# Linear attention and two expert layers: a hand-written order changed at the turning of the queries and in the first two steps

## The chip, the cores and the metric

The kernel runs on one NeuronCore of a Trainium2 chip. The metric is the device time of one execution in microseconds (us). Five engines have a queue of their own and run it in order: TensorE (PE in the profile; its weight loads are PEld), VectorE (DVE), ScalarE (ACT), GpSimd (POOL) and SyncE (SP), which here only issues DMA transfers.

## What is computed

```python
def _attn_ref(q, k, v, w_phi):            # q, k, v: (4, 8, 576, 64); w_phi: (64, 128)
    def phi(x):
        proj = np.einsum('bhsd,df->bhsf', x, w_phi)
        proj = proj - np.max(np.abs(proj), axis=-1, keepdims=True)
        return np.concatenate([np.exp(proj), np.exp(-proj)], axis=-1)
    q_p, k_p = (phi(q), phi(k))
    kv = np.einsum('bhsf,bhsd->bhfd', k_p, v)
    z = np.sum(k_p, axis=2)
    num = np.einsum('bhsf,bhfd->bhsd', q_p, kv)
    den = np.einsum('bhsf,bhf->bhs', q_p, z)[..., None] + 1e-06
    return num / den
```

Its output, as a matrix of 2304 tokens by 512, goes through a dense layer (the largest of three products with 512 x 768 matrices, then a product with a 768 x 512 matrix) and through a layer of eight experts of which each token uses two. Only the attention's part of the program is changed.

## The kernel before, in words

The attention is done in 16 steps (`NS`), one for two heads of one batch entry; a pair of steps (an even one and the odd one behind it) has the same two heads of two batch entries. Of the 576 positions 512 are a step's own; the 64 that remain (the remainder) of both steps of a pair are put together into one tile of 128 rows, kind "r", and worked on in the even step.

A step does the following. `turn` (L359) transposes the keys, the queries or the remainder on TensorE into a PSUM bank of `bank_t` (two banks), four transpositions (two for the remainder). `raw_in` (L374) copies that on ScalarE. `proj` (L380) multiplies by `w_phi` into two banks of `bank_p`, one for each group g of four tiles. On VectorE `peak` (L395) takes the largest absolute value of each row and `center` (L402) subtracts it; the subtraction also frees the bank. For keys `exp_k` (L415) makes exp(x) and exp(-x) on ScalarE. Queries are turned back once centred, by `turn_q` (L427) on TensorE, again into `bank_t`, one half (g = 0, g = 1) at a time, and `exp_q` (L434) makes the exponentials on ScalarE, which frees that bank. `kv_sum` (L448) multiplies key features by values (four products and a fifth with the remainder's features for each sign), `kv_out` copies the sums, and `numer` (L465) multiplies them by the query features in four pieces (n, h): three in a row, and the last, (1, 1), in the next period. `denom`, `den_turn`, `den_inv`, `den_back` and `divide` make the output.

The order is written by hand. `at(t, f, ...)` puts a call at a nominal time; all calls are sorted by that number, and the sorted list gives the order of each of the queues of TensorE, ScalarE, VectorE and SyncE. The number does not delay anything: what runs when is set by the queues and the semaphores. `period(base, a, b)` (L539) writes the calls for one period of 12.5: the keys and queries of step a beside the sums and numerators of step b = a - 1. `start` (L512) issues the first loads. During the attention SyncE, VectorE, ScalarE and GpSimd also convert the dense layer's weights (`narrow_load`, `narrow_mid`, `narrow_end`, `narrow_out`); GpSimd's order is the scheduler's. The tiles of transposed input (`th`), of centred values (`d`) and of loaded keys and queries have three buffers each.

Of the kernel before, what the change touches and what calls it, by code (L numbers as in the profile page):

```python
# [11 lines left out]
BF16 = mybir.dt.bfloat16  # L12
# [7 lines left out]
P = 128  # L20
# [3 lines left out]
class Plan:  # L24
# [5 lines left out]
    def at(self, t, f, *x):  # L30
        self.ops.append((t, len(self.ops), f, x))
# [7 lines left out]
def tile_linear_attention__then__moe__then__noisy_top2_moe(  # L39
# [20 lines left out]
    nc = tc.nc  # L60
# [3 lines left out]
    E, _, FF2 = e_w1.shape  # L64
# [26 lines left out]
    at = plan.at  # L91
    st, pools = {}, {}
# [197 lines left out]
    ap, ain = pools["attn"], pools["ain"]  # L290
# [17 lines left out]
    vts, rest, tiles = [], {}, {}  # L308
# [5 lines left out]
    def load_rest(bb):  # L314
        ql = ain.tile([P, H, D], F32, name="ql", bufs=1)
        kl = ain.tile([P, H, D], F32, name="kl", bufs=1)
        for t, src in ((kl, k), (ql, q)):
            for i in range(2):
                rows = slice(i * REST, (i + 1) * REST)
                dq.dma_start(t[rows], src[2 * bb + i, :, MAIN:S, :].rearrange("h p d -> p h d"))  # L320
        rest[bb] = ql, kl

    def load_rest_v(bb):
        for i in range(2):
            rows = slice(i * REST, (i + 1) * REST)
            for s in range(2):
                dq.dma_start(vls[i][rows, :, 2 * s, :],
                             v[2 * bb + i, s:H:2, MAIN:S, :].rearrange("h p d -> p h d"))

    def load_main(s):  # L330
        u, i = divmod(s, 2)
        bb, hp = divmod(u, HP)
        b = 2 * bb + i
        res = []
        for nm, src in (("km", k), ("qm", q)):
            t = ain.tile([P, 2, JT, D], F32, name=nm, bufs=3)
            dq.dma_start(t.rearrange("p h j d -> p h (j d)"),
                         src[b, 2 * hp:2 * hp + 2, 0:MAIN, :]
                         .rearrange("h (p j) d -> p h (j d)", j=JT))
            res.append(t)  # L340
        tiles[s] = res + [vts[s % 3]]

    def load_vals(s):
        u, i = divmod(s, 2)
        bb, hp = divmod(u, HP)
        b = 2 * bb + i
        vt = vts[s % 3]
        for h in range(2):
            dq.dma_start(vt[:, :, 2 * h, :],
                         v[b, 2 * hp + h, 0:MAIN, :].rearrange("(p j) d -> p j d", j=JT))  # L350
# [26 lines left out]
        nc.scalar.activation(t[:, :src.shape[1]], src, AF.Copy)  # L377
        st["t", kind] = t

    def proj(s, kind):  # L380


        t = st["t", kind]
        pj = [bank_p().rearrange("p (a f) -> p a f", a=4) for _ in range(2)]
        for jj in range(2 if kind == "r" else 4):
            for g in range(2):
                rows = slice(g * D, (g + 1) * D)
                nc.tensor.matmul(pj[g][:, jj, :], t[rows, jj, :], wphi[rows], start=True, stop=True)  # L388
        for g in range(2):
            st["pj", kind, g] = pj[g]  # L390
# [114 lines left out]
    NS = B * HP  # L505
# [4 lines left out]
            qps[s // 2, n] = ap.tile([P, 2, 2, S], F32, name=f"qp{n}", tag="qp", bufs=3)  # L510

    def start():  # L512
        warm = ap.tile([P, 1], F32, name="warm")
        nc.vector.memset(warm, 0.0)
        nc.scalar.activation(warm, warm, AF.Exp)
        load_main(0)
        for h in range(2):
            dq.dma_start(wphi[h * D:(h + 1) * D], w_phi)
        make_identity(nc, ident)
        for vt in vts:  # L520
            nc.gpsimd.memset(vt[:, :, 1, :], 1.0)
        for i in range(2):
            nc.gpsimd.memset(vls[i][(1 - i) * REST:(2 - i) * REST], 0.0)
            nc.gpsimd.memset(vls[i][i * REST:(i + 1) * REST, :, 1, :], 1.0)
        load_rest(0)
        load_vals(0)
        load_rest_v(0)
        load_main(1)
        load_vals(1)

    def step_halves(a):

        def count(a):
            return min(a, 1) + (a % 2 if a > 1 else 0)

        n = sum(count(i) for i in range(a))
        return range(n, n + count(a) if a < NS else len(halves))

    def period(base, a, b):  # L539

        def at(t, f, *x):
            plan.at(base + t, f, *x)

        if 0 < a < NS:
            at(0.0, fill, a)
            if a == 3:
                at(0.0, routing_loads)
            if a == 2:
                at(2.0, routing_consts)
            if a + 1 < NS:  # L550
                at(0.0, load_main, a + 1)
                at(0.0, load_vals, a + 1)
        if a < NS:
            if a % 2 == 0:
                at(0.0, prepare, a)
            if a + 1 == 2 * HP:
                at(0.0, load_rest, 1)
            at(0.0, turn, a, "k")
            at(0.5, raw_in, a, "k")
            at(2.7, turn, a, "q")  # L560
            at(3.2, raw_in, a, "q")
            at(3.15, proj, a, "k")
            at(4.0, peak, a, "k", 0)
            at(4.7, center, a, "k", 0)
            at(5.4, peak, a, "k", 1)
            at(6.1, center, a, "k", 1)
            for g in range(2):
                for sg in range(2):
                    at(5.3 + 1.5 * g + 0.6 * sg, exp_k, a, "k", g, sg)
            at(7.25, proj, a, "q")  # L570
            at(8.1, peak, a, "q", 0)
            at(8.8, center, a, "q", 0)
            at(9.5, peak, a, "q", 1)
            at(10.2, center, a, "q", 1)
            at(11.5, turn_q, a, "q", 0)
            at(11.95, turn_q, a, "q", 1)
            at(11.9, exp_q, a, "q", 0)
            at(12.4, exp_q, a, "q", 1)
            if a % 2 == 0:
                late = 0.0 if a else 2.1  # L580
                at(2.8 + late, turn, a, "r")
                at(3.4 + late, raw_in, a, "r")
                at(11.05, proj, a, "r")
                for g in range(2):
                    at(11.5 + 0.01 * g, peak, a, "r", g)
                    at(11.52 + 0.01 * g, center, a, "r", g)
                at(STEP + 3.0, turn_q, a, "r", 0)
                at(STEP + 3.1, exp_q, a, "r", 0)
                at(12.39, exp_k, a, "r", 0, 0)
                at(12.39, exp_k, a, "r", 0, 1)  # L590
            for n in step_halves(a):
                at(1.8 if a > 1 else 11.0, narrow_mid, n)
                at(2.8 if a > 1 else 11.5, narrow_end, n)
                at(STEP + (1.6 if a > 1 else 9.0), narrow_out, n)
            for n in step_halves(a + 1):
                at(8.0, narrow_load, n)
        if 0 < b:
            at(4.05, numer, b - 1, 1, 1)
            at(5.0, denom, b - 1, 1, 1)
            at(5.05, den_turn, b - 1, 1)  # L600
            at(6.05, den_inv, b - 1, 1)
            at(6.8, den_back, b - 1, 1)
            at(7.2, divide, b - 1, 1, 0)
            at(7.6, divide, b - 1, 1, 1)
        if 0 <= b:
# [4 lines left out]
            at(7.3, kv_out, b)  # L610
            at(8.15, numer, b, 0, 0)
# [9 lines left out]
            at(12.1, denom, b, 1, 0)  # L621

    at(0.0, start)
    for s in range(NS):
        period(s * STEP, s, s - 1)
    T = NS * STEP
# [366 lines left out]
    def overflow_table():  # L993
# [16 lines left out]
        for r in range(NREG):  # L1010
# [112 lines left out]
    for i in range(2 * 4):  # L1123
        g, j = 1 + i // 4, i % 4
        t = END + 0.1 + i * 3.2
# [207 lines left out]
```

## Time and profile before

| | |
|---|---|
| median of 3 runs | 1048.41 us (1047.31 to 1049.32) |
| the profiled execution | 1048.3 us |
| its span, first to last instruction | 1046.6 us |
| TensorE busy | 1011.4 us, 97% of the span |
| VectorE, ScalarE, GpSimd busy | 502.6, 383.7 and 314.0 us |
| TensorE busy in the first of 40 slices of the span | 7 tenths; 9 in nearly all others |
| granted TensorE clock, mean | 0.993 |

The span is what one profiled execution shows; the time of the same execution is 1.7 us longer. Busy time of TensorE counts matrix products and transpositions; idle time of the other engines costs nothing unless TensorE waits for them. A row of the timeline can stand for several instructions of one kind in a row (x4); its duration runs from the start of the first to the end of the last, and the ends of products overlap with the next ones' starts. A float32 transposition or product of 128 columns appears as one pass or two.

### The profile page before, as it was taken

The numbers are of one execution on the slowest core, as the hardware profiler recorded it, in microseconds if no ns is written. First come the engines' busy times: TensorE is split into PE (matmuls) and PEld (weight loads), VectorE is DVE, ScalarE is ACT, GpSimd is POOL, SyncE is SP. The second block draws the span as 40 slices with busy tenths as digits, with TensorE's granted clock in tenths as the row PEclk, the third lists the DMA queues.
The fourth block names the chain that finished last, engine by engine and source line by source line (L and its number), as shares of the span: only waits on it lengthen the run. The fifth ranks groups of instructions, "written<-read, shape, count | busy, mean of one in ns | idle before, by whom it ended". The sixth has DMA issues, their size and how long they took to land. (4 is left out here: it accounts for less than half of the span.)

```text
span 1046.6 us, 15778 instructions
## 1 busy us (share of the span) xinstructions
PE 1011.4 (97%) x6154; PEld 904.5 (86%) x6154; DVE 502.6 (48%) x1064; ACT 383.7 (37%) x717; POOL 314.0 (30%) x345
## 2 busy tenths in 40 slices
PE   7999999999999999999998999999999999999995
PEld 6888888889999999999997788989898979898883
DVE  2877777876524242424264616534354444444220
ACT  3666666664322222222244405323131323233110
POOL 2477654454002020202012464323233233220121
PEclk9999999999999999999999999999999999999998
DMA  6264575423300000000125435635343454542010
GB/s 189 60 192 138 146 217 186 139 86 106 96 31 1 31 2 31 1 31 1 56 96 123 149 95 181 214 104 161 114 143 135 135 167 135 159 129 74 25 64 32
DMA packets 78526, 109.21 MB, mean 104 GB/s; under 512 B 33358, under 2 KB 47822, under 8 KB 78450
## 3 DMA queue, kind: packets, MB, share of 16 engines
q1 hardware_dynamic: 67522, 78.57, 25.0%
q0 software_dynamic: 10928, 29.62, 9.1%
q8 instruction: 49, 0.80, 0.3%
q14 instruction: 27, 0.22, 0.1%
HBM read 84.77 MB, written 23.98 MB: 104 GB/s over the span
## 5 line engine op out<-in xcount | busy, mean ns | idle before, releaser
L891 PE MATMUL s<-gx,wh 128*128 128x304 f32 (+1 forms) x960 | 209.1, 309 | 0.6 <-DVE hl L902 0.6
L891 PEld LDWEIGHTS s<-gx,wh 128*128 128x128 f32 x960 | 159.0, 188 | 4.1 <-DVE hl L902 0.9
L891 PE MATMUL s<-gx,wl 128*128 128x304 f32 (+1 forms) x480 | 148.3, 309 | 0.0
L659 PE MATMUL s<-xh,wh 128*128 128x384 f32 x432 | 147.7, 342 | 0.2 <-DVE xT L502 0.2
L659 PE MATMUL s<-xh,wl 128*128 128x384 f32 x432 | 145.4, 337 | 0.0
L659 PE MATMUL s<-xl,wh 128*128 128x384 f32 x432 | 145.2, 336 | 0.0
L822 POOL DMA_INDIRECT meta<-mt,si x36 | 36.5, 1013 | 266.6 <-DVE si L818 257.5
L901 ACT ACTIVATE hh<-s 128x304 fp32r<-128x304 f32 (+1 forms) x120 | 52.1, 434 | 154.2 <-PE s L891 150.7
L122 DVE TENSOR_TENSOR wl<-raw,wh 128x1024 fp32r<-128x1024 f32 x72 | 88.0, 1223 | 40.4 <-ACT wh L121 40.3
L902 DVE SCALAR_TENSOR_TENSOR hl<-s,hh 128x304 fp32r<-128x304 f32 (+1 forms) x120 | 58.1, 488 | 96.0 <-ACT hh L901 95.9
L121 ACT ACTIVATE wh<-raw 128x1024 fp32r<-128x1024 f32 x72 | 76.0, 1056 | 58.7 <-PE p L960 19.6
L669 DVE TENSOR_TENSOR a<-s,a 128x384 f32<-128x384 f32 x72 | 40.1, 557 | 118.9 <-PE s L659 109.6
L891 PEld LDWEIGHTS s<-gx,wl 128*128 128x128 f32 x480 | 90.7, 189 | 1.4
L960 PE MATMUL p<-wh,hh 128*128 128x512 f32 (+1 forms) x216 | 87.0, 403 | 0.0
L960 PE MATMUL p<-wl,hh 128*128 128x512 f32 (+1 forms) x216 | 85.1, 394 | 0.0
L960 PE MATMUL p<-wh,hl 128*128 128x512 f32 (+1 forms) x216 | 84.9, 393 | 0.0
L659 PEld LDWEIGHTS s<-xh,wh 128*128 128x128 f32 x432 | 81.2, 188 | 2.2 <-DVE xT L502 0.6
L659 PEld LDWEIGHTS s<-xl,wh 128*128 128x128 f32 x432 | 81.2, 188 | 1.4
L659 PEld LDWEIGHTS s<-xh,wl 128*128 128x128 f32 x432 | 81.1, 188 | 0.0
L972 POOL DMA_INDIRECT out_dram<-o,emeta x40 | 44.5, 1113 | 119.8 <-DVE o L970 105.6
L398 DVE TENSOR_REDUCE m<-p 128x4 f32<-128x512 f32 (+1 forms) x80 | 49.4, 624 | 50.5 <-PE p L388 50.1
L865 POOL DMA_INDIRECT gx<-x2d,emeta x40 | 38.3, 957 | 109.0 <-PE t L876 100.4
(209 smaller groups left out, 1834.3 us busy)
## 6 DMA issues: line engine op xcount, KB each, us to landing
raw<-in_moe_w_dram SPq DMA_DIRECT2D x64, 512.0 KB, 3.8
bits<-in_moe_w_dram SPq DMA_DIRECT2D x18, 512.0 KB, 4.3
out_dram<-zrow SPq DMA_DIRECT2D x9, 512.0 KB, 5.1
x2d<-x SPq DMA_DIRECT2D x18, 256.0 KB, 2.6
km<-in_k_dram SPq DMA_DIRECT2D x16, 256.0 KB, 5.2
qm<-in_q_dram SPq DMA_DIRECT2D x16, 256.0 KB, 5.6
vt<-in_v_dram SPq DMA_DIRECT2D x32, 128.0 KB, 4.6
narrow<-nm SPq DMA_DIRECT2D x16, 256.0 KB, 2.6
```

The costliest lines, as they stand in the source:

```text
L121: nc.scalar.activation(hi, src, AF.Copy)
L122: nc.vector.tensor_tensor(lo, src, hi.bitcast(F32), op=ALU.subtract)
L398: nc.vector.tensor_reduce(m, st["pj", kind, g][:, :n], axis=AX.X, op=ALU.max, apply_absolute_value=True)
L659: nc.tensor.matmul(p_, a[:, d, fs], b_, start=(n == 0), stop=(n == 3 * KD - 1))
L669: nc.vector.tensor_tensor(a, p_, st.pop("a"), op=ALU.max)
L822: ins = nc.gpsimd.indirect_dma_start(out=meta, out_offset=bass.IndirectOffsetOnAxis(ap=si[:, t, kk:kk + 1], axis=0), in_=mt[:, t, kk, :], ...
L865: nc.gpsimd.indirect_dma_start(out=xg[:m], out_offset=None, in_=x2d[0:nrow, :], in_offset=bass.IndirectOffsetOnAxis(ap=st["meta", n][:m, i ...
L891: nc.tensor.matmul(p_, a[:, fs], b_[:, d, cs], start=(i == 0), stop=(i == 3 * KD - 1))
L901: nc.scalar.activation(hh[:, cs], p_, AF.Relu)
L902: nc.vector.scalar_tensor_tensor(hl[:, cs], p_, 0.0, hh[:, cs].bitcast(F32), op0=ALU.max, op1=ALU.subtract)
L960: nc.tensor.matmul(p_, a[:, cs], b_[:, fw], start=(r == 0), stop=(r == 3 * F2 - 1))
L972: ins = nc.gpsimd.indirect_dma_start(out=out, out_offset=bass.IndirectOffsetOnAxis(ap=mt[:m, i, 1:2], axis=0), in_=o[:m], in_offset=None, ...
```

## The change

1. In every step but the first, the first half of the queries is turned back between the second and the third numerator, and the second half behind the third (nominal times 9.95 and 11.05 instead of 11.5 and 11.95). The exponentials follow at 10.5 and 11.5, both ahead of the third numerator's denominator. The remainder's projection moves from 11.05 to 11.4.
2. The calls for step 0 and for the keys and queries of step 1 up to their projections are no longer written by `period` but by a new function `opening`, in another order: the remainder is turned before the first projection, its projection goes to two idle banks of `bank_s`, and the projection of step 0's queries to one bank of each kind; step 1's keys are turned before step 0's sums.
3. `load_main` can load the keys or the queries alone. The queries of step 0 and the keys of step 1 are loaded behind the remainder, the queries of step 1 behind the values.
4. `busy(n)` multiplies a tile of zeros (`idle`, two-byte numbers, 256 columns) by itself n times into the bank of `bank_k`: 12 times at the beginning, 4 times in front of the first `kv_sum`.

```diff
-    def proj(s, kind):
+    def proj(s, kind, banks=(bank_p, bank_p)):
...
-        pj = [bank_p().rearrange("p (a f) -> p a f", a=4) for _ in range(2)]
+        pj = [bank().rearrange("p (a f) -> p a f", a=4) for bank in banks]
...
     def start():
+        st["idle"] = ap.tile([P, 256], BF16, name="idle")
+        nc.vector.memset(st["idle"], 0.0)
...
-        load_main(0)
+        load_main(0, 0)
...
         load_rest(0)
+        load_main(0, 1)
+        load_main(1, 0)
         load_vals(0)
         load_rest_v(0)
-        load_main(1)
+        load_main(1, 1)
         load_vals(1)
+
+    def busy(n):
+
+        t = bank_k()
+        for _ in range(n):
+            nc.tensor.matmul(t[:, :256], st["idle"][:, :P], st["idle"], start=True, stop=True)
...
-            at(11.5, turn_q, a, "q", 0)
-            at(11.95, turn_q, a, "q", 1)
-            at(11.9, exp_q, a, "q", 0)
-            at(12.4, exp_q, a, "q", 1)
+            at(9.95, turn_q, a, "q", 0)
+            at(10.5, exp_q, a, "q", 0)
+            at(11.05, turn_q, a, "q", 1)
+            at(11.5, exp_q, a, "q", 1)
...
-                at(11.05, proj, a, "r")
+                at(11.4, proj, a, "r")
...
+    def opening():
+
+        at(1.2, busy, 12)
+        at(4.0, turn, 0, "k")
...
+        at(11.0, busy, 4)
...
     at(0.0, start)
+    opening()
```

TensorE at the beginning, before (km and qm are a step's keys and queries, kl and ql those of the remainder; t, p, s and k are the kinds of PSUM bank):

```order
L371 MATMUL t<-ident,km 128x128 x4
L371 MATMUL t<-ident,qm 128x128 x4
L388 MATMUL p<-wphi,th 128x128 x8
L371 MATMUL t<-ident,kl 128x128
L371 MATMUL t<-ident,ql 128x128
L388 MATMUL p<-wphi,th 128x128 x12
L431 MATMUL t<-ident,d 128x128 x8
```

And TensorE at the same place in the changed program, where the lines' numbers are one to a few higher:

```order
L540 MATMUL k<-idle 128x256
L372 MATMUL t<-ident,km 128x128 x4
L372 MATMUL t<-ident,kl 128x128
L372 MATMUL t<-ident,ql 128x128
L389 MATMUL p<-wphi,th 128x128 x8
L372 MATMUL t<-ident,qm 128x128 x4
L389 MATMUL s<-wphi,th 128x128 x4
```

The first row is the last of twelve products of zeros; the remainder's two transpositions stand ahead of the first projection, and the remainder's projection (the last row) goes to banks of kind s.

TensorE at the end of a period with an even step a, before (the six rows of L469 are numerators of the step ahead, qp the query features, d centred values, vt and vl values):

```order
L388 MATMUL p<-wphi,th 128x128 x8
L469 MATMUL s<-qp_395,kv 128x288 x6
L388 MATMUL p<-wphi,th 128x128 x4
L431 MATMUL t<-ident,d 128x128 x8
L371 MATMUL t<-ident,km 128x128 x4
L457 MATMUL k<-vt_109,kp_837 128x128 x4
L457 MATMUL k<-vl_111,kp_923 128x128
```

And TensorE there in the changed program:

```order
L389 MATMUL p<-wphi,th 128x128 x8
L470 MATMUL s<-qp_156,kv 128x288 x4
L432 MATMUL t<-ident,d 128x128 x4
L470 MATMUL s<-qp_156,kv 128x288 x2
L432 MATMUL t<-ident,d 128x128 x4
L389 MATMUL p<-wphi,th 128x128 x4
L372 MATMUL t<-ident,km 128x128 x4
L458 MATMUL k<-vt_110,kp_493 128x128 x4
L458 MATMUL k<-vl_111,kp_585 128x128
```

The eight transpositions of the queries are split around the third numerator, and the remainder's projection now follows them.

ScalarE at the same place, before (dn are denominators, kp the remainder's key features, th a copy of transposed input):

```order
L478 ACTIVATE dn<-s 64x288 x2
L440 ACTIVATE qp_394<-t 128x2x256 x2
L478 ACTIVATE dn<-s 64x288
L421 ACTIVATE kp_563<-d 128x2x128 x2
L440 ACTIVATE qp_394<-t 128x2x256 x2
L377 ACTIVATE th<-t 128x512
```

And ScalarE there in the changed program:

```order
L479 ACTIVATE dn<-s 64x288 x2
L441 ACTIVATE qp_414<-t 128x2x256 x4
L479 ACTIVATE dn<-s 64x288
L422 ACTIVATE kp_585<-d 128x2x128 x2
L378 ACTIVATE th<-t 128x512
```

Both halves' exponentials stand together, ahead of the third denominator and of the remainder's key features.

## Rows read from the trace of the kernel before

**Rows 1.** Stretches (first: until step 2's keys turn): busy PE, PEld, DVE, ACT, POOL; clock.
```profile
0.00:34.04 34.04, 25.77 (x161) 21.69 (x161) 14.15 (x26) 14.98 (x32) 6.81 (x34) 1.00 0.53 149
62.93:234.50 171.57, 163.44 (x1312) 141.78 (x1313) 134.74 (x273) 112.57 (x244) 97.00 (x79) 1.00 0.52 155
245.00:1046.60 801.60, 784.23 (x4391) 707.76 (x4390) 321.22 (x705) 229.45 (x387) 183.96 (x214) 0.99 0.30 91
```

**Rows 2.** Waits of PE, 25 to 230 us: total us, times, longest.
```profile
PE t L371 <- ACT qp L440: 10.3, 14, 0.7
```

**Rows 3.** Timeline, TensorE in the opening: start, us, instruction, idle time before.
```profile
3.99 1.08 PE L371 MATMUL t<-ident,km 128*128 128x128 f32 x4 [3.99 <-DMA km<-in_k_dram]
8.77 0.45 PE L371 MATMUL t<-ident,ql 128*128 128x128 f32 x1 [0.42 <-DMA ql<-in_q_dram]
18.93 1.11 PE L371 MATMUL t<-ident,km 128*128 128x128 f32 x4 [0.32 <-ACT qp L440]
19.84 1.91 PE L457 MATMUL k<-vt,kp 128*128 128x128 f32 x8
21.97 1.33 PE L457 MATMUL k<-vt,kp 128*128 128x128 f32 x8
24.11 1.16 PE L388 MATMUL p<-wphi,th 64*128 64x128 f32 x16
```

**Rows 4.** Timeline, the other engines in the opening.
```profile
1.44 0.46 SPq L337 DMA_DIRECT2D qm<-in_q_dram  x1
4.56 1.31 SPq L320 DMA_DIRECT2D ql<-in_q_dram  x2
5.11 0.60 ACT L377 ACTIVATE th<-t 128x512 f32<-128x512 f32 x1 [2.67 <-PE t L371]
7.97 0.69 DVE L398 TENSOR_REDUCE m<-p 128x4 f32<-128x512 f32 x1 [6.89 <-PE p L388]
```

**Rows 5.** The page's DMA issues: times, KB each, median us to landing.
```profile
qm<-in_q_dram SPq DMA_DIRECT2D x16, 256.0 KB, 5.6
```

**Rows 6.** Timeline, end of a period with an even step.
```profile
72.18 3.18 PE L469 MATMUL s<-qp,kv 128*128 128x288 f32 x12
74.49 0.69 DVE L413 TENSOR_TENSOR d<-p,m 128x512 f32<-128x512 f32 x1
75.29 0.72 PE L388 MATMUL p<-wphi,th 64*128 64x128 f32 x8
75.94 1.09 PE L431 MATMUL t<-ident,d 128*128 128x128 f32 x8
76.25 0.72 DVE L398 TENSOR_REDUCE m<-p 128x2 f32<-128x256 f32 x2
76.63 1.08 ACT L440 ACTIVATE qp<-t 128x512 f32<-128x512 f32 x2 [1.80 <-PE t L431]
76.89 0.74 DVE L413 TENSOR_TENSOR d<-p,m 128x256 f32<-128x256 f32 x2
77.77 0.66 PE L371 MATMUL t<-ident,km 128*128 128x128 f32 x4 [0.74 <-ACT qp L440]
78.05 0.71 ACT L421 ACTIVATE kp<-d 128x256 f32<-128x256 f32 x2
79.16 0.39 PE L457 MATMUL k<-vl,kp 128*128 128x128 f32 x2
```

**Rows 7.** Timeline, end of the next period, with an odd step.
```profile
87.03 3.18 PE L469 MATMUL s<-qp,kv 128*128 128x288 f32 x12
87.95 0.69 DVE L413 TENSOR_TENSOR d<-p,m 128x512 f32<-128x512 f32 x1
89.28 0.40 ACT L478 ACTIVATE dn<-s 64x288 f32<-64x288 f32 x1 [0.50 <-PE s L469]
90.05 1.04 PE L431 MATMUL t<-ident,d 128*128 128x128 f32 x8
91.82 0.66 PE L371 MATMUL t<-ident,km 128*128 128x128 f32 x4 [0.74 <-ACT qp L440]
```

More of the change, by code (lines that the diff above doesn't have):

```diff
@@ L328, in load_rest_v, with load_main @@
                              v[2 * bb + i, s:H:2, MAIN:S, :].rearrange("h p d -> p h d"))
-    def load_main(s):
+    def load_main(s, which=None):
         u, i = divmod(s, 2)
@@ L333, in load_main @@
         b = 2 * bb + i
-        res = []
-        for nm, src in (("km", k), ("qm", q)):
+        res = tiles.setdefault(s, [])
+        for nm, src in (("km", k), ("qm", q))[slice(which, which if which is None else which + 1)]:
             t = ain.tile([P, 2, JT, D], F32, name=nm, bufs=3)
@@ L340, in load_main @@
             res.append(t)
-        tiles[s] = res + [vts[s % 3]]
+        if len(res) == 2:
+            res.append(vts[s % 3])
     def load_vals(s):
@@ L552, in period @@
                 at(0.0, load_vals, a + 1)
-        if a < NS:
-            if a % 2 == 0:
-                at(0.0, prepare, a)
+        if a < NS and a % 2 == 0:
+            at(0.0, prepare, a)
+        if 1 < a < NS:
             if a + 1 == 2 * HP:
@@ L570, in period @@
             at(7.25, proj, a, "q")
+        if 0 < a < NS:
             at(8.1, peak, a, "q", 0)
@@ L574, in period @@
             at(10.2, center, a, "q", 1)
-            at(11.5, turn_q, a, "q", 0)
-            at(11.95, turn_q, a, "q", 1)
-            at(11.9, exp_q, a, "q", 0)
-            at(12.4, exp_q, a, "q", 1)
+            at(9.95, turn_q, a, "q", 0)
+            at(10.5, exp_q, a, "q", 0)
+            at(11.05, turn_q, a, "q", 1)
+            at(11.5, exp_q, a, "q", 1)
             if a % 2 == 0:
-                late = 0.0 if a else 2.1
-                at(2.8 + late, turn, a, "r")
-                at(3.4 + late, raw_in, a, "r")
-                at(11.05, proj, a, "r")
+                at(2.8, turn, a, "r")
+                at(3.4, raw_in, a, "r")
+                at(11.4, proj, a, "r")
                 for g in range(2):
@@ L590, in period @@
                 at(12.39, exp_k, a, "r", 0, 1)
+        if a < NS:
             for n in step_halves(a):
@@ L604, in period @@
             at(7.6, divide, b - 1, 1, 1)
-        if 0 <= b:
+        if 0 < b:
             at(0.45, kv_sum, b, 0)
@@ L610, in period @@
             at(7.3, kv_out, b)
+        if 0 <= b:
             at(8.15, numer, b, 0, 0)
@@ L621, in period @@
             at(12.1, denom, b, 1, 0)
+    def opening():
+        at(1.2, busy, 12)
+        at(4.0, turn, 0, "k")
+        at(4.5, raw_in, 0, "k")
+        at(4.5, turn, 0, "r")
+        at(5.2, raw_in, 0, "r")
+        at(5.3, proj, 0, "k")
+        at(6.2, turn, 0, "q")
+        at(6.8, raw_in, 0, "q")
+        at(7.0, proj, 0, "r", (bank_s, bank_s))
+        at(8.2, proj, 0, "q", (bank_p, bank_s))
+        at(9.5, turn, 1, "k")
+        at(10.2, raw_in, 1, "k")
+        at(11.0, busy, 4)
+        for g in range(2):
+            at(7.0 + 1.4 * g, peak, 0, "k", g)
+            at(7.7 + 1.4 * g, center, 0, "k", g)
+            at(10.0 + 0.01 * g, peak, 0, "r", g)
+            at(11.0 + 0.01 * g, center, 0, "r", g)
+            at(12.0 + 1.4 * g, peak, 0, "q", g)
+            at(12.7 + 1.4 * g, center, 0, "q", g)
+            at(15.2 + 1.4 * g, peak, 1, "k", g)
+            at(15.9 + 1.4 * g, center, 1, "k", g)
+            for sg in range(2):
+                at(9.4 + 1.3 * g + 0.6 * sg, exp_k, 0, "k", g, sg)
+                at(17.0 + 3.0 * g + 0.6 * sg, exp_k, 1, "k", g, sg)
+        for sg in range(2):
+            at(12.0 + 0.4 * sg, exp_k, 0, "r", 0, sg)
+        at(12.45, kv_sum, 0, 0)
+        at(14.1, turn_q, 0, "r", 0)
+        at(14.2, turn, 1, "q")
+        at(14.8, exp_q, 0, "r", 0)
+        at(14.9, raw_in, 1, "q")
+        at(14.9, proj, 1, "k")
+        at(15.4, turn_q, 0, "q", 0)
+        at(15.9, exp_q, 0, "q", 0)
+        at(15.9, kv_sum, 0, 1)
+        at(18.2, kv_out, 0)
+        at(18.2, turn_q, 0, "q", 1)
+        at(18.7, exp_q, 0, "q", 1)
+        at(18.7, proj, 1, "q")
     at(0.0, start)
+    opening()
     for s in range(NS):
```

## The prediction

> **What bounds the kernel now.** I read the stretches first [rows 1]. From 245 us on TensorE is busy for 784.2 of 801.6 us; in the steady part of the attention, 62.93 to 234.50 us, for 163.4 of 171.6; in the first 34.04 us only for 25.8. VectorE, the next busiest, has 134.7 of 171.6 in the steady part. So TensorE's queue sets the end: what it waits less in the attention the whole rest should move up by, because behind the attention there is nearly no idle time to swallow it. The list of waits names one cause between 25 and 230 us [rows 2]: `turn` of the next keys (L371) waits 14 times for the exponentials of turned queries (L440), 10.3 us in all. The timeline shows why [rows 6]: both halves of the queries are turned at 75.94, the next keys need the PSUM bank of the first half, and ScalarE frees it only at 77.71 (76.63 + 1.08).
>
> The opening has two troubles [rows 3, 4]. It follows one long path with few things beside it: the keys of step 2 are turned at 34.04, though TensorE worked only 25.8 us. And TensorE is at the lower of its two levels, 1.2 and 2.4 GHz, until about 22 us: four transpositions take 1.08 us at 3.99 and 1.11 at 18.93, but 0.66 at 77.77; eight products take 1.91 at 19.84, 1.33 at 21.97. The column of the granted clock says 1.00 there [rows 1], so only the durations show it. The level stayed low although the engine ran from 3.99 to 8.35 (8.77 less 0.42) without a wait that matters; it rose when it had run since 18.93 without one.
>
> **The steady steps.** Times are those of the trace, with the new order laid over them. A 128-column pass costs 0.116 us: from 77.77 to 79.16 there are four transpositions and eight passes of products [rows 6]. So four transpositions cost 0.46, `kv_sum` (20 passes) 2.3, one numerator 1.01 (three from 87.03 to 90.05, [rows 7]).
>
> Odd step: two numerators end at 89.05; the first half has been centred at 88.64 (87.95 + 0.69), so its turn doesn't wait. The turn ends at 89.51, the third numerator at 90.52, the second half at 90.98. ScalarE comes to the first half's exponentials when the second denominator is copied, 89.68 (89.28 + 0.40), and, 0.69 after the turn began (as 75.94 to 76.63), at 89.74; with 1.08 they end at 90.8. The next keys turn at 90.98 instead of 91.82: 0.84 gained, with a margin of only 0.2 to a new wait.
>
> Even step: the remainder's projection now stands behind the second half. 72.18 + 2.02 + 0.46 + 1.01 (second half centred at 75.18, in time) + 0.46 = 76.13, plus 0.65 for the projection (75.29 to 75.94) = 76.78: the keys turn 0.99 earlier. But what is late next is the remainder's key features. The projection ends at 76.85 (0.72 long), VectorE's two maxima and subtractions can begin at 76.9 instead of 76.25, last 1.38 (76.25 to 77.63), and end at 78.3; half of ScalarE's 0.71 makes the first sign ready at 78.7. The fifth product of `kv_sum` wants it at 76.78 + 1.39 = 78.17. It waits 0.55, and everything on TensorE stands behind it. Against 79.16 it starts at 78.72: 0.44 is left of the 0.99.
>
> From the turn of step 2's keys on there are seven changes from an even to an odd step and six from odd to even: 7 x 0.44 + 6 x 0.84 = 8.1 us. VectorE has room: in the even step it falls behind by 0.65, in a step that has 36.8 us idle in 171.6 [rows 1], about 3 us a step.
>
> **The opening.** SyncE issues the remainder's queries one issue earlier (the 0.46 of the queries at 1.44 goes behind them); they landed for 8.77, so now at about 8.2. But TensorE now transposes them ahead of the first projection, which waits with them: 0.1 for the transposition, 1.2 for the projection [rows 3], first maximum at 9.5 instead of 7.97. Then, at the higher level: maximum and subtraction 1.4 (0.69 for either) to 10.9, which frees the bank for the projection of the queries, 1.1 to 12.0; turn of step 1's keys, the result 0.69 later; ScalarE copies it (0.60) before the second group's first exponential, which I take to be as long: 13.9. From there TensorE is the path: `kv_sum` 2.3, remainder's queries 0.23, turn of queries 0.46, projection 1.1, half turn 0.46, `kv_sum` 2.3, half turn 0.46, projection 1.1, three numerators 3.02, two half turns 0.92: together 12.35, so step 2's keys turn at 26.2 (13.9 + 12.35). VectorE is ready beside it: step 1's four key operations end about 2.9 after that projection, and TensorE needs 3.2 to come back. That is 7.8 us gained on 34.04.
>
> At the lower level the terms on TensorE double. From 8.4: projection 2.2, turn 0.92, remainder's projection 1.3, projection 2.2, turn 0.92, to 15.9; the result, copy and exponential to 17.3; `kv_sum` 4.6 to 21.9; if the level rises only there, as it does today, the remaining 10.05 end at 31.9: 2.1 us gained. Rows of before don't say when it rises in an order that leaves TensorE with almost no wait from 8.3 to 17. I take the middle of the two ends, 5.0.
>
> What hides the rest: the products of zeros have no row. A 256-column product of two-byte numbers lies between one pass of 0.116 and four at the lower level, 0.93 (estimates from the pass above), with a weight load inside: twelve end between 2.6 and 12.4 us. Up to about 6.5 they are free, since the projection waits for the remainder's queries; the row nearest in columns, two passes at the lower level (0.46), ends at 6.7, so I cost them at nothing. The four later ones stand in front of a `kv_sum` that waits until 13.9 while TensorE comes free at 12.5: at 0.23 each, the higher level, 0.9 is hidden in 1.4; at 0.46 they run from 15.9 to 17.8 against 17.3, 0.5 us lost, which I leave to the range. Clearing the tile costs VectorE nothing before 9.5. The queries of step 1 are issued behind all the values, at about 10.4, and wanted at 16.4: with the 5.6 us from issue to landing [rows 5] they arrive at 16.0, so a wait of up to 1 us is possible here.
>
> Sum: 8.1 + 5.0 = 13.1 us off the profiled 1048.3 (its span 1046.6 and 1.7 around it); the median of the runs, 1048.4, is the same within 0.1. That gives 1035.2 us.
>
> **Rivals.**
> 1. The level rises early, by the zeros, and stays through the wait for the remainder's queries. Then the opening gives 7.8, in all 15.9: 1032.4. For it: TensorE would run from about 1.2 to 6 instead of from 3.99. Against it: 3.99 to 8.35 didn't raise it. The Trainium skill (TensorE: Matmul & The Clock Gate, Part 1) says that the low level is the default and activity releases it, and it speaks of how busy the array is, not of values; by that rule zeros serve as well. The trace agrees on the rise at 22 us and shows nothing of zeros.
> 2. The steady gain is taken back. The wait for a bank only changes its place: the fifth product in even steps, the tight 0.2 in odd ones, and VectorE, whose maxima start earlier behind the same work. Where it takes back all 8.1, the opening's 5.0 remains: 1043.3. For it: I already find 0.55 of 0.99 gone in even steps. Against it: nothing of this kind shows in odd steps.
> 3. Slower: the first half's turn now stands in TensorE's queue before the third numerator, and if VectorE centres that half late, TensorE stops there in every step. It has 0.41 us to spare. The gain of 13.1 us is 0.87 for each of 15 steps, so the time is slower than before from a centre that is 1.3 us later; at 1.6 later it is 15 x 1.2 - 13.1 = 5 us slower, 1053. Against it: VectorE's order inside a step is the same, and the steps repeat to a hundredth.
> 4. The change does not do what it says: the zeros cost what the opening saves, and the bank wait stays. 1048.4.
>
> **How the numbers follow.** The forecast with the level's rise anywhere between the ends, 1032.4 to 1038.1 (its own range), 0.63; rival 1 at its end or below, 0.18; rival 2, 0.10; rival 3, 0.04; rival 4, 0.05. A difference of 0.2%, 2.1 us, is about what a measurement of this kernel can tell. Faster: 0.63 + 0.18 + 0.10 = 0.91; same 0.05; slower 0.04. The range holds the forecast and rival 1, with 2 us more below for a fifth product that waits less than 0.55, and 3 us above for waits at the tight places: 1030.5 to 1041.0; the rest of rival 2 and the others stay out, 0.19.
>
> **What would show it.** Right: the keys of step 2 turn at 26 to 32 us; no wait of L372 for the exponentials of queries in odd steps; a new wait of about 0.55 of the remainder's product in `kv_sum`, seven times, for ScalarE; pairs of steps at about 27.6 us instead of 28.89 (62.93 to 91.82); the first projection at 8.3; transpositions below 0.7 us well before 20. Wrong: pairs of steps as long as before, a wait in front of the first half's turn, transpositions of 1.1 us still at 25, or new idle time of TensorE behind 245.

## The result and the profile after

The changed kernel takes 1036.59 us (median of 4 runs, 1036.25 to 1037.04); the kernel before took 1048.05 us beside it (1047.31 to 1049.32). The ratio is 0.989, with a 95% interval of 0.9873 to 0.9907. The forecast was 1035.2 us. The profiled execution took 1036.27 us with a span of 1034.6 us, 12.0 us less than the span before.

The same stretches as in [rows 1]: until the keys of step 2 are turned, the steady part from the turn of step 4's keys, and a rest that begins 4.27 us behind the first product of the dense layer, as 245 us did before.

```profile
0.00:29.20 29.20, 24.10 (x176) 19.85 (x177) 13.03 (x25) 14.36 (x31) 6.42 (x33) 0.88 0.63 173
56.90:222.31 165.41, 162.60 (x1317) 142.24 (x1316) 143.49 (x275) 115.52 (x245) 101.59 (x79) 1.00 0.54 162
...
232.81:1034.60 801.79, 784.43 (x4391) 707.34 (x4389) 320.43 (x703) 229.06 (x387) 181.86 (x213) 0.99 0.29 91
```

The opening is 4.84 us shorter, the steady stretch 6.16 us; TensorE's idle time in the latter fell from 8.1 us (171.57 less 163.44) to 2.8. The rest is as long as before, within 0.2 us.

The waits of TensorE until 240 us (total us, times, longest), against [rows 2]:

```profile
PE k L458 <- ACT kp L422: 3.3, 7, 0.5
PE t L372 <- DMA kl<-in_k_dram: 1.8, 1, 1.8
PE t L372 <- DMA ql<-in_q_dram: 1.6, 1, 1.6
PE k L540 <- DVE warm L517: 1.3, 1, 1.3
PE k L458 <- ACT kp L426: 0.3, 1, 0.3
```

The 10.3 us for the exponentials of the queries are gone. In their place stands the wait that the prediction named: the fifth product of `kv_sum` for the remainder's key features (the first row), 7 times, 3.3 us. In the opening TensorE now waits for the remainder's two loads.

The end of a period with an even step, against [rows 6], in the timeline (start, duration in us, instruction, idle time before), first TensorE:

```profile
68.16 0.60 PE L432 MATMUL t<-ident,d 128*128 128x128 f32 x4
68.59 1.14 PE L470 MATMUL s<-qp,kv 128*128 128x288 f32 x4
69.56 0.60 PE L432 MATMUL t<-ident,d 128*128 128x128 f32 x4
70.09 0.71 PE L389 MATMUL p<-wphi,th 64*128 64x128 f32 x8
70.74 0.66 PE L372 MATMUL t<-ident,km 128*128 128x128 f32 x4
72.76 0.49 PE L458 MATMUL k<-vl,kp 128*128 128x128 f32 x2 [0.47 <-ACT kp L422]
```

and the other engines at the same place:

```profile
68.79 1.09 ACT L441 ACTIVATE qp<-t 128x512 f32<-128x512 f32 x2
70.84 0.76 DVE L399 TENSOR_REDUCE m<-p 128x2 f32<-128x256 f32 x2 [0.58 <-PE p L389]
71.51 0.74 DVE L414 TENSOR_TENSOR d<-p,m 128x256 f32<-128x256 f32 x2
72.29 0.72 ACT L422 ACTIVATE kp<-d 128x256 f32<-128x256 f32 x2 [0.57 <-DVE d L414]
```

The turns and the third numerator follow each other without a gap. ScalarE has freed the first half's bank at 69.88 (68.79 + 1.09), so the next keys turn at 70.74 without a wait; then the chain from the projection (70.09) over maximum, subtraction and exponential makes the fifth product late. In the odd step nothing waits: the keys of step 6 turn here, 0.44 us behind the second half:

```profile
84.18 0.60 PE L432 MATMUL t<-ident,d 128*128 128x128 f32 x4
84.62 0.60 PE L372 MATMUL t<-ident,km 128*128 128x128 f32 x4
```

A pair of steps takes 27.71 us (56.91 to 84.62) instead of 28.89.

TensorE in the opening, against [rows 3] (chosen rows):

```profile
1.27 2.74 PE L540 MATMUL k<-idle 128*128 128x256 bf16 x12 [1.27 <-DVE warm L517]
3.96 0.92 PE L372 MATMUL t<-ident,km 128*128 128x128 f32 x4
6.70 0.30 PE L372 MATMUL t<-ident,kl 128*128 128x128 f32 x1 [1.82 <-DMA kl<-in_k_dram]
8.64 0.45 PE L372 MATMUL t<-ident,ql 128*128 128x128 f32 x1 [1.63 <-DMA ql<-in_q_dram]
9.02 2.08 PE L389 MATMUL p<-wphi,th 64*128 64x128 f32 x16
11.03 1.11 PE L372 MATMUL t<-ident,qm 128*128 128x128 f32 x4
14.91 0.66 PE L372 MATMUL t<-ident,km 128*128 128x128 f32 x4
29.20 0.60 PE L372 MATMUL t<-ident,km 128*128 128x128 f32 x4
```

and the granted clock (first of the last three numbers) in stretches of it:

```profile
5.00:7.00 2.00, 0.30 (x1) 0.14 (x1) 0.00 (x0) 0.52 (x1) 1.93 (x14) 1.00 0.85 191
7.00:9.00 2.00, 0.37 (x2) 0.18 (x1) 0.00 (x0) 0.00 (x0) 0.47 (x5) 0.75 0.96 294
9.00:11.00 2.00, 2.00 (x17) 1.79 (x16) 0.00 (x0) 0.38 (x1) 0.00 (x0) 0.50 0.85 192
14.80:17.00 2.20, 1.83 (x13) 1.24 (x12) 2.09 (x5) 1.33 (x3) 0.00 (x0) 0.99 1.00 341
```

The first transposition of a group is the one to read: kl at 6.70 takes 0.30 us, the higher level; ql at 8.64 takes 0.45, the lower. In this execution the level rose while TensorE multiplied zeros and turned keys, and fell again within the two waits of 1.8 and 1.6 us. The column, which stood at 1.00 through the low level before, shows this fall: 0.50 is 1.2 of 2.4 GHz. Projection and turn then take 2.08 and 1.11 us, until the level comes back at about 14.8.

Behind the attention a small part is lost. Three places serve as markers in every run: the first product of the dense layer, the first turn of gathered rows (TensorE waits there for GpSimd's gather), and the expert product that follows the split of hidden values `hl`.

| us | dense layer | gathered rows | product behind hl | end of span |
|---|---|---|---|---|
| before | 240.73 | 565.61 (+324.88) | 643.13 (+77.52) | 1046.6 (+403.5) |
| after | 228.54 | 552.98 (+324.44) | 631.08 (+78.10) | 1034.6 (+403.5) |

12.19 us gained at the first marker are 12.05 at the third. What TensorE waits for between the second and the third marker has changed:

```profile
554.41 1.09 PE L933 MATMUL t<-ident,gx 128*128 128x128 f32 x4 [0.80 <-DMA gx<-x2d,emeta]
631.08 0.54 PE L948 MATMUL s<-gx,wh 128*128 128x304 f32 x2 [0.23 <-DVE hl L959]
```

The first is a second wait for gathered rows, of 0.80 us, which the kernel before doesn't have; the wait for hl was 0.63 us before.

### The profile page after: what moved, and what is told of

It reads as the page before. It is cut to its first block, busy times and chain, and to the rows that moved or that the text cites. A ratio compares the mean times of both kernels' runs of the same rounds, so it can differ in the third digit from the quotient of the medians.

```text
span 1034.6 us, 15800 instructions
## 1 busy us (share of the span) xinstructions
PE 1008.9 (98%) x6170; PEld 903.0 (87%) x6170; DVE 511.3 (49%) x1065; ACT 386.0 (37%) x717; POOL 316.7 (31%) x345
## 5 line engine op out<-in xcount | busy, mean ns | idle before, releaser
L470 PE MATMUL s<-qp,kv 128*128 128x288 f32 x240 | 68.6, 419 | 0.0
```

The source lines that it names most:

```text
L470: nc.tensor.matmul(p_, st["kv", s][:, 2 * h + sg, :], qps[u, i][:, h, sg, n * HALF:(n + 1) * HALF], start=(sg == 0), stop=(sg == 1))
```

## The experiments

The numbers in brackets behind a time are the lowest and highest run; the ratio is to the kernel before on the same chip, with its 95% interval.

**Each part alone.** The new steady order in the kernel before, from step 1 on:

```diff
-            at(11.5, turn_q, a, "q", 0)
-            at(11.95, turn_q, a, "q", 1)
+            if a:
+                at(9.95, turn_q, a, "q", 0)
+                at(10.5, exp_q, a, "q", 0)
+                at(11.05, turn_q, a, "q", 1)
...
-                at(11.05, proj, a, "r")
+                at(11.4 if a else 11.05, proj, a, "r")
```

Expected: 

> Only part 1 of the change, from step 1 on (halves of the queries turned around the third numerator, the remainder's projection behind them); the opening is that of before and there are no products of zeros. Theory (the two parts add, and the steady steps carry the larger one): pairs of steps take 27.7 us instead of 28.9, the wait of the next keys for the exponentials is gone in all 14 places and 0.47 us of wait stands at the fifth product seven times; 8.4 us off, 1039.6 us. Rival (the steady gain hangs on the opening, because loads or weight conversions fall behind without it): less than 5 us off, above 1043, with new idle time in front of TensorE that a DMA or GpSimd ends.

Measured: 1040.27 us (1039.31 to 1041.16), 0.992 [0.9904, 0.9937]. The waits of TensorE, of the fifth product and of the next keys:

```profile
PE k L457 <- ACT kp L421: 3.3, 7, 0.5
...
PE t L371 <- ACT qp L440: 0.3, 1, 0.3
```

Step 2's keys turn at 32.30, the dense layer starts at 231.66: 9.07 us gained, 1.74 of them in the opening, so 7.3 in the steady part. Of the 1.74, 0.83 are there before the new order begins (the projection that starts at 24.11 in [rows 3] starts at 23.28): in this execution the level rose once early, kl taking 0.33 at 7.71, and was back sooner. The rest is step 1's. The time is 8.3 us off the kernel before on the same chip, 8.4 expected; the theory held, with 0.8 of it by the level.

The opening alone: the changed kernel with the old numbers of the steady order.

```diff
-            at(9.95, turn_q, a, "q", 0)
+            at(11.5, turn_q, a, "q", 0)
...
-                at(11.4, proj, a, "r")
+                at(11.05, proj, a, "r")
```

Expected: 

> Only parts 2 to 4 (the new opening, the loads' order, the products of zeros); the halves of the queries and the remainder's projection stand as before in every step. Theory: step 2's keys turn at about 30 us instead of 34.04 (29.2 as in the changed kernel plus the bank wait of about 0.85), then pairs of steps of 28.9 as before; 4.0 us off, 1044.0 us. Rival (the opening's gain is given back later, since everything behind is bound elsewhere): within 1 us of before.

Measured: 1045.46 us (1044.85 to 1046.05), 0.9968 [0.9957, 0.998], 1.5 us more than expected. The bank wait is back:

```profile
PE t L372 <- ACT qp L441: 10.3, 14, 0.7
```

Step 2's keys turn at 29.05 and the dense layer starts at 235.74, 4.99 us earlier; but the product behind hl comes 79.35 us after the gathered rows instead of 77.52, and 1.8 us are lost there: TensorE waits 1.49 us for hl instead of 0.63. Up to the dense layer the parts add up: 7.3 + 5.0 = 12.3, and the whole has 12.19; the moment at which the level rises, which differs between these executions, moves the opening by up to 1 us.

**What the zeros do.** Both calls of `busy` are taken out:

```diff
-        at(1.2, busy, 12)
...
-        at(11.0, busy, 4)
```

Expected: 

> The changed kernel without any product of zeros (12 and 4 left out). Theory: the twelve raise TensorE's level at about 4.7 us, but the wait for the remainder's queries lets it fall again before 8.6, so that they buy only the two cheap transpositions in between; the rise near 15 us comes from the engine's run from 8.6 on. Then transpositions take 1.08 at 4 us and 0.45 to 0.47 each at 6.7, the rest is alike, and the time is 1036.6, within 0.7 us. Rival (the zeros are what brings the level up at 15): the level rises later, at up to 22 us, and the time is 1 to 3 us longer, 1037.6 to 1039.6.

Measured: 1036.47 us (1035.64 to 1037.12), 0.9884 [0.9867, 0.99]: the time of the changed kernel. Without zeros the remainder's keys are turned at the lower level, and the projection runs at it as with them:

```profile
6.51 0.45 PE L372 MATMUL t<-ident,kl 128*128 128x128 f32 x1 [1.50 <-DMA kl<-in_k_dram]
9.02 0.45 PE L372 MATMUL t<-ident,ql 128*128 128x128 f32 x1 [2.06 <-DMA ql<-in_q_dram]
9.40 2.08 PE L389 MATMUL p<-wphi,th 64*128 64x128 f32 x16
```

Step 2's keys turn at 29.60, 0.4 us later than in the changed kernel, but the remainder's queries also landed 0.4 later here (9.02 for 8.64). As they are placed, the sixteen products of zeros buy nothing that the times show: where the level rises, the rise is lost before there is work for it. So the next kernel puts 28 more into the waits for the remainder:

```diff
+        at(4.4, busy, 28)
```

Expected: 

> The changed kernel with 28 more products of zeros between the turn of step 0's keys and the turn of the remainder, where TensorE waits for the remainder's queries until 8.6 us. Theory: the level that the first twelve raise at about 4.7 us then stays, the first projection takes 1.2 instead of 2.1 us, step 2's keys turn at about 26.5 instead of 29.2, and 2.7 us come off the changed kernel: 1033.9. Rival (products of zeros don't hold the level, or the extra ones end late): the 28 take 0.23 each, end at 11 us and delay the first projection by 2 us: 1037 to 1039.

Measured: 1033.79 us (1033.58 to 1034.77), 0.9857 [0.9841, 0.9874]. It beats both kernels; the version without zeros took 2.7 us more on the same chip, and their runs don't overlap. TensorE in its opening:

```profile
3.84 1.09 PE L372 MATMUL t<-ident,km 128*128 128x128 f32 x4
4.72 4.12 PE L540 MATMUL k<-idle 128*128 128x256 bf16 x28
8.68 0.27 PE L372 MATMUL t<-ident,kl 128*128 128x128 f32 x1
...
8.99 1.16 PE L389 MATMUL p<-wphi,th 64*128 64x128 f32 x16
...
27.12 0.60 PE L372 MATMUL t<-ident,km 128*128 128x128 f32 x4
```

The projection takes 1.16 instead of 2.08 us and step 2's keys turn 2.08 us earlier. The keys ahead of the 28 are turned at the lower level (1.09 us for four), the remainder's behind them at the higher (0.27 for one). So zeros raise the level and hold it, as other products do. That is the rule of the Trainium skill (TensorE: Matmul & The Clock Gate, Part 1) that the prediction cited, which speaks of how busy the array is and not of values; these rows agree.

**Not waiting for the remainder.** Its turn goes behind the first projection:

```diff
-        at(4.5, turn, 0, "r")
-        at(5.2, raw_in, 0, "r")
...
+        at(5.4, turn, 0, "r")
+        at(5.5, raw_in, 0, "r")
```

Expected: 

> The changed kernel with the remainder turned behind the first projection instead of ahead of it (as before the change), all else alike. Theory (the wait of the first projection for the remainder's queries is a price of the new opening): the first projection starts at 5.6 instead of 9.0, at the raised level, the first maximum at 6.9 instead of 11.1; the engine still waits for the remainder's queries afterwards, the level falls again, and step 2's keys turn at 28.0 instead of 29.2: 1.2 us off the changed kernel, 1035.3; if the level stays, 3 us off, 1033.5. Rival (VectorE's chain from the remainder on sets the end, so where the first projection stands is without effect): 1036.5.

Measured: 1036.52 us (1035.22 to 1036.99), 0.9882 [0.9864, 0.9899]; no gain. The time is the rival's, but not for the rival's reason.

```profile
5.57 2.08 PE L389 MATMUL p<-wphi,th 64*128 64x128 f32 x16 [0.69 <-ACT th L378]
...
27.50 0.60 PE L372 MATMUL t<-ident,km 128*128 128x128 f32 x4
```

The opening did what was expected, although the level stayed low in this execution: step 2's keys turn 1.70 us earlier, and so does the dense layer's start (226.84). All of it is lost later: the stretch from the gathered rows to the product behind hl is 80.03 instead of 78.10 us, with 1.70 us of wait for hl instead of 0.23.

**The fifth product.** Two attempts to have the remainder's key features ready earlier. In the first the remainder's projection goes between the third numerator and the second half, and the exponentials are called earlier:

```diff
-                at(11.4, proj, a, "r")
+                at(11.02, proj, a, "r")
...
-                at(12.39, exp_k, a, "r", 0, 0)
+                at(11.45, exp_k, a, "r", 0, 0)
```

In these two kernels the remainder's key features are made from values ahead of their subtraction. Expected: 

> The changed kernel with the remainder's projection between the third numerator and the second half's turn, and the remainder's key features on ScalarE between the two halves' exponentials. Theory (the wait at the fifth product of kv_sum, 7 times 0.47 us, is the rest of the price of part 1): these waits go, no other takes their place, pairs of steps take 27.2 instead of 27.7 us, 3.3 us off: 1033.2. Rival (VectorE or the second half's exponentials are just behind): the wait turns up at the projection of the keys or the next turn, less than 1 us off, above 1035.6.

Measured: 1040.38 us (1038.92 to 1041.62), 0.9921 [0.9903, 0.9938]; missed. The same with the 28 zeros, expected: 

> Both: 28 products of zeros in the wait for the remainder's queries, and the remainder's projection and key features moved ahead as in the run on the fifth product. Theory (the opening and the steady steps add): 2.8 + 3.3 us off the changed kernel, 1030.5. Rival (they share a limit): no better than the better of the two, 1033.

Measured: 1036.63 us (1035.0 to 1039.05), 0.9893 [0.9875, 0.9911]; missed as well. The fifth product doesn't wait in them, but since the exponentials now stand ahead of the subtraction, the buffers of centred values are freed in another order, and a projection waits for VectorE three times (here of the first):

```profile
PE p L389 <- DVE d L414: 3.4, 3, 1.1
```

So their times don't test the theory. In the pairs of steps behind 113 us, where no projection waits, a pair takes 27.26 us, and the theory said 27.2; but that is with features that need not wait for their subtraction. The second attempt moves the whole chain, the reciprocal of the denominators too, which would stand in front of it on VectorE:

```diff
-                at(11.4, proj, a, "r")
+                at(11.02, proj, a, "r")
...
-                    at(11.5 + 0.01 * g, peak, a, "r", g)
-                    at(11.52 + 0.01 * g, center, a, "r", g)
+                    at(11.1 + 0.01 * g, peak, a, "r", g)
+                    at(11.12 + 0.01 * g, center, a, "r", g)
...
-                at(12.39, exp_k, a, "r", 0, 0)
+                at(11.45, exp_k, a, "r", 0, 0)
...
-            at(11.3, den_inv, b, 0)
+            at(11.06, den_inv, b, 0)
```

Expected: 

> The changed kernel with the remainder's projection between the third numerator and the second half's turn, the two small denominator operations and the remainder's maxima and subtractions right behind on VectorE, and the remainder's key features on ScalarE between the two halves' exponentials, behind the subtractions that they read. Theory (the wait at the fifth product of kv_sum, 7 times 0.47 us, is the rest of the price of part 1): the wait goes, pairs of steps take 27.2 instead of 27.7 us, the keys of step 15 turn about 2.8 us earlier, and 2 to 3.3 us come off the changed kernel, as far as the waits behind 550 us pass it on: 1033.3 to 1034.6. Rival (the next limit is at once behind): the wait turns up at another product or turn, pairs stay above 27.5 us.

Measured: 1040.62 us (1039.44 to 1042.26), 0.9918 [0.9905, 0.9932]: 4 us slower than the changed kernel. TensorE in the attention:

```profile
71.51 0.49 PE L458 MATMUL k<-vl,kp 128*128 128x128 f32 x2
...
73.84 0.33 PE L432 MATMUL t<-ident,d 128*128 128x128 f32 x1 [0.29 <-ACT th L378]
```

The fifth product is only some 0.2 us late now, but ScalarE, which makes the features ahead of the exponentials of the queries' second half, comes later to the copy of the next keys, and the turn of the remainder's queries waits 0.3 for it, 7 times. Pairs of steps take 27.82 us, 0.1 longer than without this edit; the dense layer starts at 228.25. So the gain inside the attention is nil, as the rival had it. The 4 us are lost behind it: 2.75 to the product behind hl (a stretch of 80.85 us) and 1.65 later (405.2). TensorE there:

```profile
633.82 0.88 PE L948 MATMUL s<-gx,wh 128*128 128x304 f32 x2 [2.07 <-DVE hl L959]
634.75 0.71 PE L948 MATMUL s<-gx,wh 128*128 128x304 f32 x2
...
637.50 0.44 PE L948 MATMUL s<-gx,wh 128*128 128x304 f32 x2
```

The 1.65 us are the level's: it fell in that wait, the granted clock is 0.50 from 633.8 to 637.0 us, and 3.2 us at half the clock cost 1.6. The first attempt without the 28 zeros shows the same (a wait of 2.42 us, a granted clock of 0.57 from 633.6 to 637.0, 1.55 us lost); in two other kernels the level stayed through 2.13 and 2.28 us of the same wait, and nothing was lost behind it. VectorE in this kernel:

```profile
631.50 0.75 DVE L1027 SCALAR_TENSOR_TENSOR o<-p,emeta,pv 128x512 f32<-128x512 f32 x1 [3.33 <-DMA gx<-x2d,emeta]
```

With the 28 zeros, expected: 

> The same, and the 28 products of zeros in the wait for the remainder's queries. Theory (opening and steps add): the keys of step 15 turn 2.1 + 2.8 us earlier than in the changed kernel, near 204.4, and the time is 1030.5 to 1032. Rival (the chain of GpSimd's gathers behind 550 us sets the end as soon as TensorE arrives earlier): the keys of step 15 turn as early, but the time stays at 1033 to 1034 with longer waits behind 550 us.

Measured: 1035.53 us (1035.12 to 1035.99), 0.987 [0.9855, 0.9886]; missed, no steady gain again (step 15's keys turn at 207.90). With the remainder behind the projection and the zeros split around it, 5 and 14, expected: 

> The same with the remainder behind the first projection; the products of zeros are split, 5 in front of that projection and 14 behind it, where the engine waits for the remainder's queries. Theory: the first maximum at 7 us, the keys of step 2 turn at 25.5 to 26.5, those of step 15 near 203, 1 us before the run with 28 zeros in a row; 1029.5 to 1031.5. Rival (as before, the gathers take it back): no difference from that run within 0.7 us.

Measured: 1035.4 us (1034.19 to 1036.04), 0.9866 [0.9851, 0.9881]; the theory missed. It is 0.1 us from the run before it, as the rival had it. Its opening is the best of all, step 2's keys at 25.90 and the dense layer at 225.87, but the stretch from the gathered rows to the product behind hl is 80.02 us and takes it back.

**The loss behind the attention.** First the wait for the gathered rows: one more block of the dense layer's second product goes ahead of the first turn of gathered rows, so that TensorE has work there.

```diff
-        if i == 2:
+        if i == 0:
```

Expected: 

> The changed kernel with one block of the dense layer's second product moved ahead of the first turn of the gathered rows near 550 us, where TensorE waits 3.6 us for the gather and then runs its next products at the lower level. Theory (after the attention's gain the wait for the gather is 0.3 to 1 us longer and the fall of the level costs more than before, which is where some of the gain went): the 2.1 us of that block cover more than half of the wait, the level doesn't fall, 1 to 3 us off: 1034.5. Rival (the gather's end is set by TensorE's own earlier work, or the four turns in a row now wait for their banks as long): within 0.7 us of 1036.5.

Measured: 1036.75 us (1036.29 to 1037.21), 0.9887 [0.9869, 0.9904]; the time is the rival's. The waits of TensorE from 245 us on:

```profile
PE t L933 <- DMA gx<-x2d,emeta: 3.1, 4, 1.0
PE s L948 <- DVE hl L959: 2.1, 1, 2.1
```

The wait is cut in four and its sum is 3.1 instead of 3.6; and the wait for hl grows from 0.2 to 2.1. From the first marker to the third this kernel takes 403.96 us, the changed kernel 402.54; an opening that was 0.8 us shorter in this execution hides half of the loss.

Then the other place: VectorE's `o`, an expert's product, scaled, plus the previous outputs. In the kernel before and in the changed one it stands at

```profile
640.81 0.75 DVE L970 SCALAR_TENSOR_TENSOR o<-p,emeta,pv 128x512 f32<-128x512 f32 x1 [1.89 <-DMA pv<-out_dram,ic]
...
628.75 0.75 DVE L1027 SCALAR_TENSOR_TENSOR o<-p,emeta,pv 128x512 f32<-128x512 f32 x1 [1.49 <-DMA gx<-x2d,emeta]
```

and needs the previous outputs (pv) that GpSimd gathers, issued at 623.76 in the changed kernel, 5.0 us ahead (the second row puts the wait down to the gather of gx, but `o` reads p, emeta and pv, and the first row names pv). In the slow version above `o` came 6.8 us after the issue. The splits that TensorE needs are queued behind `o`. The last kernel is the one with 28 zeros, and asks for this gather ahead of the next expert's rows:

```diff
-            tp = g0 + 12.0
+            tp = g0 + (0.15 if n == 1 else 12.0)
```

Expected: 

> The kernel with 28 more products of zeros in the wait (1033.79 us), in which GpSimd issues the gather of the previous outputs of expert 1 (pv) ahead of the next expert's rows instead of behind three of them, and VectorE makes its index ahead of the splits of hidden values. Theory: part of what the attention gains is lost at about 631 us because VectorE's o stands at 627.3 waiting for that gather (issued at 621.7, idle 2.05 us before o), and the splits of weights and of hidden values that TensorE needs stand behind o. Then the index comes at about 615, the gather lands before 621, o runs straight behind the splits at about 625, TensorE's wait for hl (0.8 us here, 1.0 to 2.4 in the versions with the remainder's features moved) goes to nothing, and the stretch from the first turn of gathered rows to the product that waited for hl falls from 78.8 to 77.9 or less: 1032.9 us. Rival A: o is not what TensorE waits behind; the gather is earlier and the wait of 0.8 stays: 1033.8. Rival B: the gather stands in GpSimd's queue ahead of the next expert's rows and waits there for the scatters of expert 0; those rows come later, and TensorE's turn of them, which waits 0.7 today, waits 1 to 2 us more: 1035 to 1036.

Measured: 1034.18 us (1032.85 to 1034.39), 0.9848 [0.9835, 0.9861], beside 1049.52 for the kernel before; 1032.9 was expected. VectorE at the same place:

```profile
624.70 1.16 DVE L122 TENSOR_TENSOR gx<-t,gx 128x512 fp32r<-128x512 f32 x2 [2.68 <-issue]
625.77 0.74 DVE L1028 SCALAR_TENSOR_TENSOR o<-p,emeta,pv 128x512 f32<-128x512 f32 x1
```

`o` has no idle time before it, the wait of TensorE for hl (0.8 in the kernel with 28 zeros) is gone from the list, and the stretch from the gathered rows is 78.34 instead of 78.79, half of what was expected; the first turn of gathered rows ran at the lower level here (1.09 instead of 0.63 us), which is the other half. That TensorE's wait for hl hangs on this gather is shown; its gain can't be told in the time (the two intervals overlap).

## Why the prediction was right, and where it was not

- **TensorE's queue sets the end, and the rest moves up.** Right: 12.19 us gained at the dense layer, 12.0 at the end of the span. It holds less exactly than the prediction put it: "nearly no idle time to swallow it" is true of the totals, but the stretch between the second and the third marker was 0.6 to 3.8 us longer than before in every kernel that ran. In the changed kernel the waits in it grew by 0.4 us, by the second wait for gathered rows (0.80), while the wait for hl fell from 0.63 to 0.23; in the slower versions the wait for hl, behind `o` and its gather, is the larger part (up to 2.42 us).
- **The steady steps.** The waits, their cause and how often they come were right. Even step: the next keys turn 1.01 us earlier (14.84 to 13.83), 0.99 forecast. The fifth product starts 2.02 us behind that turn (70.74 to 72.76) instead of 1.39, so it loses 0.63, 0.55 forecast. Odd step: from there to the next keys 11.86 us instead of 12.66, 0.80 gained against 0.84. So 7 x 0.38 + 6 x 0.80 = 7.5 us; most of what is missing is in the first term, 2.7 instead of 3.1. From step 2's keys to the dense layer the trace has 12.19 - 4.84 = 7.35. The forecast was 8.1.
- **The opening.** 4.84 us against the middle of 5.0, step 2's keys at 29.20. That these agree so closely is partly luck: the middle is not what either end described. The remainder's queries landed for 8.64, not 8.2, and the first projection started at 9.02, not 8.3. The level did rise early in this execution, as rival 1 had it, and did not stay; it came back at about 14.8, between the two ends. The argument against an early rise, that 3.99 to 8.35 didn't raise the level, was one execution's: in the first experiment, whose opening is that of before, kl takes 0.33 at 7.71, behind transpositions and a projection alone. Three of the kernels above have the same opening as the changed kernel (the two attempts at the fifth product without the 28 zeros, and the moved block). There the level didn't rise early at all (kl takes 0.45 us), yet it came by about 13.3, and step 2's keys turn at 28.27 to 28.65, 5.4 to 5.8 us earlier than before.
- **The zeros cost nothing.** Right for the time, and they brought nothing: the kernel without them has the same time. Rival 1's time, 1032.4, needed zeros through the wait as well; with 28 there the runs gave 1033.8.
- **Rival 2**, the wait that only changes its place, took 0.63 of 0.99 in even steps and nothing in odd ones. It came true in full for the next edit, the one that should have freed the fifth product. **Rival 3** did not come: no wait stands in front of the first half's turn.
- **What is left.** Forecast 13.1, profiled 12.0, medians 11.5: 0.7 from the steady term, 0.2 from the opening, 0.2 behind the attention; the last 0.5 lie within the spread of the runs.

Open is why `o` comes 5.0 to 7.2 us after the pv gather's issue. It is 5.8 to 7.2 in the seven kernels where GpSimd issues this gather 1.6 to 2.0 us behind the gather of rows ahead of it, and 5.0 to 6.3 in the six, the kernel before among them, where 2.8 to 3.1 us lie between. That its transfer then queues behind theirs is not shown.

## What to carry to other kernels

When a wait is removed, work out when the next thing in that queue has its operands: here 0.63 of 0.99 us went to it, and a second attempt to free it only moved the wait to another engine. If an engine is to be kept at its higher clock, fill its waits up to the work that needs it; a rise ahead of a wait can be lost in the wait. And follow a gain through the rest of the program by markers at the same instructions, since an engine that works in order behind a transfer can swallow it hundreds of microseconds later.

## What the runs showed of the hardware that was not expected

- Products of zeros raise TensorE's level and hold it: behind 28 more of them the first projection takes 1.16 us in all four kernels that have them in a row; with the first twelve alone it takes 2.08 in all six. In the changed kernel the level fell through two waits of 1.8 and 1.6 us (granted clock 0.75, then 0.50).
- The rise is not always at the same time. Behind the same twelve zeros the four transpositions of the first keys take 0.75 us in one kernel (the last one with a split), 0.92 in the changed kernel and 1.06 to 1.09 in the others, and kl, at 6.6 to 6.7, takes 0.30 or 0.31 in two kernels and 0.45 in three.
- A wait of 2.07 and one of 2.42 us near 631 lost the level, for 3.2 and some 3 us; waits of 2.13 and 2.28 us at the same place did not.
- The granted clock showed 1.00 in the opening before although transpositions took nearly twice their later time (1.08 us for four, 0.66 later); it showed the fall to 0.50 once the level had risen. For this program's beginning the durations have to be read.
